# Dealing the keys of a decode attention to the 128 partitions in another order

## The chip, the cores and the metric

The kernel runs on one core of a Trainium2 chip. The metric is the device time of one execution in microseconds (us); the median of three runs before the change is 1363.97 us (1363.89 to 1364.12). The time after the change is compared with it.

## What is computed

One token goes through a layer norm, and then through attention over a long cache and a gated feed-forward block side by side; both results are added to the token. All is float32. Cut to what matters:

```python
# x: [1, 1, 576]; 32 heads of 128; the caches hold 16384 keys a head
xn = layernorm(x)                                    # eps 1e-5
q = (xn @ wq).reshape(1, 1, 32, 128).transpose(0, 2, 1, 3)
scores = einsum("bhqd,bhkd->bhqk", q, k_cache) * 128 ** -0.5
o = einsum("bhqk,bhkd->bhqd", softmax(scores), v_cache)
a = o.transpose(0, 2, 1, 3).reshape(1, 1, 4096) @ wo
b = (gelu(xn @ w_gate) * (xn @ w_up)) @ w_down       # 576 -> 4608 -> 576
out = x + a + b
```

k_cache and v_cache are [1, 32, 16384, 128]. A head's K is 16384 x 128 x 4 bytes = 8.39 MB, and so is its V; 32 heads make 536.87 MB of the 587.6 MB that the kernel reads. In memory the 16384 keys of a head lie one behind the other, 512 bytes each.

Neither the softmax nor the sum over keys asks which key lies in which partition: every order is as good as another, as long as K and V of a head are dealt in the same way.

## The kernel before, in words

**Slots.** Three buffers of 128 partitions x 16384 floats (64 KB in each partition, 8.39 MB in all) hold everything that is streamed: slot_a and slot_b (`sa`, `sb`) take the K of odd and even heads in turn, slot_v (`sv`) takes V. Before the heads they hold the weights of the projections, and after them w_down and wo.

**The deal of the keys.** With P = 128 and R = 16384 / 128 = 128, line 176 makes the views `kv` and `vv` of the caches, in which partition p holds the keys 128p to 128p + 127, that is a block of 128 keys or 64 KB that is contiguous in memory. The block of partition p + 1 follows it. One transfer (lines 352 and 355) moves one head's K or V: 128 blocks of 64 KB, one into each partition.

**One head.** VectorE multiplies the whole K in place by q, which stands in all partitions (line 396), and sums each key's 128 products (line 398), which gives the scores as 128 x 128: partition by key within the block. Then come the maximum (lines 387 to 389, with a transpose on TensorE at line 375), the exponential on ScalarE (line 427) and 32 matmuls of 128 x 512 over V (issued by `chain`, line 337), in which TensorE sums over the partitions. ScalarE takes the result out of PSUM (line 420).

**The order of the transfers.** SyncE (SP) issues all of them from one queue. After the weights of the projections it issues head 0's K in two halves of 64 keys a block (lines 358 and 359, by `load`), then head 1's K and head 0's V, then a loop over pairs of heads. In it, `take` (line 341) waits for a semaphore and lowers it again:

```python
take(nc.sync, s_kf)          # VectorE has read the slot's last K
load_k(i * 2 + (2 + s), dst, s)
take(nc.sync, s_vf)          # TensorE has read the last V
load_v(i * 2 + (1 + s))
```

So a K transfer is issued when VectorE is done with the K two heads back, and a V transfer when TensorE is done with the V before it; SP issues them in just this order, and a wait holds up all that stands behind it. VectorE, ScalarE and TensorE run loops of their own over the heads and meet through semaphores; VectorE's wait for a K of line 396, and TensorE's for V, are for all 16 counts that the 16 DMA engines give when a transfer has landed.

**The end.** While the last two heads are worked on, SP loads w_down and wo into the K slots, and TensorE adds their products up; four small transfers write the 576 outputs.

Of the kernel before, what the change touches and what calls it, by code (L numbers as in the profile page):

```python
# [13 lines left out]
P = 128  # L14
H, SK, DH = 32, 16384, 128
D, DF = 576, 4608
R = SK // P
SUB = 64
# [99 lines left out]
@with_exitstack  # L118
def kernel(ctx: ExitStack, tc: tile.TileContext, x, k_cache, v_cache, wq, wo, wg, wu, wd, out):
    nc = tc.nc  # L120
    ends = tc.alloc_semaphore("ends")
    slots = []
    for i, name in enumerate(("slot_a", "slot_b", "slot_v")):
        t = nc.alloc_sbuf_tensor_at(name, [P, R * DH], F32, offset=SLOT_AT + i * SLOT_B)
        SIZES[t.name] = R * DH
        slots.append(t.ap())
    i = nc.sync.dma_start(slots[0], wq[:DM].rearrange("(p j) f -> p (j f)", j=DJ)).then_inc(ends, 64)
    tc.no_tile_sem_insts.add(i.ins.name)
    tc.add_to_no_dep_group("first", i.ins)
    tc.declare_fence(nc.sync.nop().ins, group="first")  # L130
    with tc.tile_critical(sync_engine=mybir.EngineType.SP):
        decode(tc, x, k_cache, v_cache, wq, wo, wg, wu, wd, out, slots, ends)
    tc.no_sync_barrier()
    nc.sync.wait_ge(ends, 64)
# [19 lines left out]
def decode(tc, x, k_cache, v_cache, wq, wo, wg, wu, wd, out, slots, s_ends):  # L154
    nc = tc.nc
# [4 lines left out]
    def sem():  # L160
        return tc.alloc_semaphore(f"d{next(names)}")
# [11 lines left out]
        SIZES[t.name] = 512 * banks  # L173
        return t.ap()

    kv, vv = (c.rearrange("b h (p n) d -> p (b h) (n d)", p=P) for c in (k_cache, v_cache))
    xf = x.rearrange("b s d -> (b s) d")
    of = out.rearrange("b s d -> (b s) d")
    wmain = {n: w[:DM].rearrange("(p j) f -> p (j f)", j=DJ) for n, w in (("q", wq), ("g", wg), ("u", wu))}
# [4 lines left out]
    sa, sb, sv = slots  # L184
# [34 lines left out]
    def load(dst, src, again=False, **kw):  # L219
        if again:  # L220
            o.dma(dst, src, spent.pop(0), value=32, **kw)
        else:
            s = sem()
            o.dma(dst, src, s, **kw)
            if kw.get("eng") != "scalar":
                spent.append(s)
        return dst
# [13 lines left out]
    for i in range(2):  # L241
# [6 lines left out]
    s_q, s_m, s_n, s_o, s_e, s_v, s_po, s_pq, s_pt, s_pb, s_pc, s_vf, s_kf, s_qf, s_qd, s_d, s_a = (  # L248
        tc.alloc_semaphore(f"h{n}") for n in range(17))
    s_k = [tc.alloc_semaphore(f"k{n}") for n in range(2)]  # L250
# [92 lines left out]
    def head(h):  # L343
        return bass.ds(h, 1)
# [4 lines left out]
    o.wait("scalar", [qb], [z, qs, nb, pe, lsum, oall, qcur])  # L349

    def load_k(h, dst, s):
        nc.sync.dma_start(dst, kv[:, head(h), :].rearrange("p h f -> p (h f)")).then_inc(s_k[s], 16)

    def load_v(h):
        nc.sync.dma_start(sv, vv[:, head(h), :].rearrange("p h f -> p (h f)")).then_inc(s_v, 16)

    parts = [(sb[:, i * SUB * DH : (i + 1) * SUB * DH], S[:, i * SUB : (i + 1) * SUB]) for i in range(R // SUB)]
    for i, (dst, _) in enumerate(parts):
        load(dst, kv[:, 0, i * SUB * DH : (i + 1) * SUB * DH])
    o.wait("sync", [], [sa])  # L360
    load_k(1, sa, 1)
    o.wait("sync", [], [sv])
    load_v(0)
    with nc.sync.Fori(0, (H - 2) // 2) as i:
        for s, dst in ((0, sb), (1, sa)):
            take(nc.sync, s_kf)
            load_k(i * 2 + (2 + s), dst, s)
            take(nc.sync, s_vf)
            load_v(i * 2 + (1 + s))
# [71 lines left out]
    for j in range(1, WD_A):  # L441
        dve("scalar_tensor_tensor", total, first[j], hT[:, j : j + 1], total, op0=ALU.mult, op1=ALU.add)
    take(nc.sync, s_vf)
    load_v(H - 1)
    take(nc.sync, s_kf)
    wd_rows = load_rows(sa, 0, wdv, WD_A, WD_T - WD_A)
# [86 lines left out]
```

## Time and profile before

| | |
|---|---|
| median of 3 runs | 1363.97 us (1363.89 to 1364.12) |
| the profiled execution's own time | 1363.89 us |
| its span, first to last instruction | 1362.1 us |
| time around the span | 1.8 us |
| bytes read from memory | 587.60 MB |
| VectorE (DVE) busy | 1158.7 us, 85% of the span |
| TensorE (PE) busy, modelled | 444.3 us, 33% |
| ScalarE (ACT) busy | 67.8 us, 5% |

The profile is of one execution. It gives each engine's busy time, groups of instructions by source line, what ended an engine's idle time, and for the 16 DMA engines the share of time in which they had a packet under way and the bytes that they moved. A transfer's "us to landing" runs from its issue on SP until its data is there, and so holds the time in which it queued behind earlier transfers.

### The profile page before, as it was taken

How to read it: one execution, taken by the hardware profiler on the slowest of the kernel's cores; microseconds unless marked ns; L12 is line 12 of the kernel's file. 1: busy time of each engine (PE TensorE's matmuls, PEld its weight loads, DVE VectorE, ACT ScalarE, POOL GpSimd, SP SyncE). 2: the span in 40 equal slices, each digit the busy share in tenths (PEclk: the TensorE clock that was granted, in tenths of full speed). 3: DMA queues.
4: the chain of work that ended last, by engine and by line, in shares of the span. 5: the costliest groups of instructions: out<-in, count | busy, mean ns of one | idle time of the engine just before them, and what ended most of it. 6: DMA issues, size and time to landing. Idle time of an engine off the chain costs nothing. (4 is left out here: it accounts for less than half of the span.)

```text
span 1362.1 us, 7778 instructions
## 1 busy us (share of the span) xinstructions
PE 444.3 (33%) x3012; PEld 161.5 (12%) x3012; DVE 1158.7 (85%) x195; ACT 67.8 (5%) x234; POOL 1.0 (0%) x7
## 2 busy tenths in 40 slices
PE   2431233333322333323223333233223333232236
PEld 1110111100110111101111111011011111011012
DVE  1069999999888888899888888998888888988882
ACT  0000000000000000000000000000000000000000
POOL 0000000000000000000000000000000000000000
PEclk9775666666556666666556666665566666655668
DMA  9999999999999999999999999999999999999998
GB/s 401 447 424 435 446 433 435 431 431 433 433 433 431 435 445 435 435 431 431 433 433 433 431 435 445 437 433 431 433 431 433 433 431 435 446 435 433 430 432 349
DMA packets 11827, 587.69 MB, mean 431 GB/s; under 512 B 1319, under 2 KB 1325, under 8 KB 1710
## 3 DMA queue, kind: packets, MB, share of 16 engines
q1 hardware_dynamic: 11812, 587.60, 99.7%
q8 instruction: 5, 0.08, 0.0%
q10 hardware_dynamic: 10, 0.01, 0.0%
HBM read 587.60 MB, written 0.00 MB: 431 GB/s over the span
## 5 line engine op out<-in xcount | busy, mean ns | idle before, releaser
L337 PE MATMUL po<-slot_v,pe 128*4 128x512 f32 x2048 | 292.0, 734 | 580.9 <-PEq L341 580.9
L396 DVE TENSOR_TENSOR slot_a<-slot_a,qs 128x16384 f32<-128x16384 f32 x16 | 275.6, 17226 | 34.9 <-DVEq L341 34.9
L396 DVE TENSOR_TENSOR slot_b<-slot_b,qs 128x16384 f32<-128x16384 f32 x15 | 258.4, 17226 | 32.5 <-DVEq L341 32.5
L398 DVE TENSOR_REDUCE scores<-slot_a 128x128 f32<-128x16384 f32 x16 | 275.5, 17220 | 2.3
L398 DVE TENSOR_REDUCE scores<-slot_b 128x128 f32<-128x16384 f32 x15 | 258.3, 17220 | 2.2
L337 PEld LDWEIGHTS po<-slot_v,pe 128*4 128x4 f32 x2048 | 56.4, 98 | 789.4 <-issue 789.4
L375 PE MATMUL pg<-ident,pm 128*1 128x128 f32 x32 | 11.9, 372 | 238.3 <-PEq L341 238.3
L420 ACT ACTIVATE z<-po 128x512 f32<-128x512 f32 x32 | 19.1, 597 | 831.0 <-ACTq L341 831.0
L337 PE MATMUL pc<-same,z 128*128 128x1 f32 x256 | 59.8, 355 | 0.0
L337 PEld LDWEIGHTS pc<-same,z 128*128 128x128 f32 x256 | 57.1, 328 | 0.5
L210 DVE TENSOR_TENSOR slot_v<-pg,same 128x396 f32<-128x396 f32 (+1 forms) x6 | 3.3, 558 | 52.1 <-PE pg L207 51.9
L375 PEld LDWEIGHTS pg<-ident,pm 128*1 128x1 f32 x32 | 2.5, 79 | 243.6 <-issue 243.6
L389 DVE TENSOR_REDUCE nm<-pg 1x1 f32<-1x128 f32 x32 | 8.9, 279 | 21.5 <-DVEq L341 21.5
L337 PE MATMUL pg<-nm,ones 1*128 1x1 f32 x64 | 17.7, 343 | 18.5 <-PEq L341 18.5
L337 PE MATMUL pqs<-qcur,ones 1*128 1x128 f32 x64 | 14.8, 312 | 25.3 <-PEq L341 25.3
L210 DVE SCALAR_TENSOR_TENSOR slot_b<-slot_b,hT 128x576 f32<-128x576 f32 x27 | 22.1, 819 | 0.9
L337 PEld LDWEIGHTS pg<-nm,ones 1*128 1x128 f32 x64 | 15.9, 307 | 27.9 <-issue 27.9
L425 ACT ACTIVATE nb<-pg 128x1 f32<-128x1 f32 x32 | 5.5, 171 | 240.5 <-ACTq L341 240.5
L210 DVE TENSOR_REDUCE scores<-slot_b 128x64 f32<-128x8192 f32 x2 | 17.4, 8686 | 0.1
L210 DVE TENSOR_TENSOR slot_b<-slot_b,qs 128x8192 f32<-128x8192 f32 x2 | 17.4, 8688 | 0.0
L387 DVE TENSOR_REDUCE pm<-scores 128x1 f32<-128x128 f32 x32 | 9.1, 285 | 8.2 <-DVEq L341 8.0
L337 PEld LDWEIGHTS pqs<-qcur,ones 1*128 1x128 f32 x64 | 9.6, 187 | 53.9 <-issue 53.9
(81 smaller groups left out, 133.6 us busy)
## 6 DMA issues: line engine op xcount, KB each, us to landing
slot_b<-in_A_k_cache_dram SPq DMA_DIRECT2D x2, 4096.0 KB, 24.1
slot_b<-in_B_w_down_dram SPq DMA_DIRECT2D x1, 8064.0 KB, 42.0
slot_b<-in_B_w_gate_dram SPq DMA_DIRECT2D x1, 6912.0 KB, 55.1
slot_a<-in_B_w_up_dram SPq DMA_DIRECT2D x1, 6912.0 KB, 37.8
slot_a<-in_A_wo_dram SPq DMA_DIRECT2D x1, 3456.0 KB, 41.0
slot_v<-in_B_w_gate_dram SPq DMA_DIRECT2D x1, 2304.0 KB, 28.8
slot_v<-in_B_w_up_dram SPq DMA_DIRECT2D x1, 2304.0 KB, 37.2
slot_a<-in_B_w_down_dram SPq DMA_DIRECT2D x1, 2304.0 KB, 28.1
```

Source lines behind the costliest of these rows:

```text
L210: o.op("vector", lambda e: getattr(e, name)(out, *ins, **kw), out, *[a for a in ins if isinstance(a, bass.AP)], *[a for a in kw.values() i ...
L337: i = nc.tensor.matmul(dst, lhs, rhs, start=start, stop=stop)
L375: nc.tensor.transpose(pt[:1, :P], pm, ident).then_inc(s_pt, 1)
L387: nc.vector.reduce_max(pm, sc, axis=AX.X).then_inc(s_m, 1)
L389: nc.vector.tensor_reduce(nm[:1], pt[:1, :P], axis=AX.X, op=ALU.max, negate=True).then_inc(s_n, 1)
L396: nc.vector.tensor_mul(blk, blk, qs.unsqueeze(1).to_broadcast([P, R, DH])).then_inc(s_d, 1)
L398: nc.vector.tensor_reduce(sc, blk, axis=AX.X, op=ALU.add).then_inc(s_d, 1)
L420: nc.scalar.activation(z, PO, AF.Copy).then_inc(s_o, 1)
L425: nc.scalar.activation(nb, pb[:, :1], AF.Copy, scale=SCALE).then_inc(s_a, 1)
```

## The change

The blocks stay what they are, 128 keys or 64 KB contiguous in memory. What changes is the partition into which each goes. The index of a block was the partition p. It is now split as 16j + e, with e from 0 to 15 and j from 0 to 7, and the view has e outside and j inside, so partition 8e + j holds block 16j + e. A transfer's source is now a pattern of 16 (step 64 KB) by 8 (step 1 MB) blocks, where it was one of 128 blocks with a step of 64 KB; its destination is still the slot's 128 partitions in order. Eight partitions that follow one another thus hold blocks 1 MB apart, and 16 partitions with a distance of 8 hold blocks that are neighbours. K and V are dealt alike, so the computation on the chip is the same, with its sums over the partitions in another order. Number and size of the transfers, the waits, the loops and every instruction of the compute engines stay as they were.

```diff
-    kv, vv = (c.rearrange("b h (p n) d -> p (b h) (n d)", p=P) for c in (k_cache, v_cache))
+    kv, vv = (c.rearrange("b h (j e n) d -> e j (b h) (n d)", e=16, j=P // 16) for c in (k_cache, v_cache))
...
     def load_k(h, dst, s):
-        nc.sync.dma_start(dst, kv[:, head(h), :].rearrange("p h f -> p (h f)")).then_inc(s_k[s], 16)
+        nc.sync.dma_start(dst, kv[:, :, head(h), :].rearrange("e j h f -> e j (h f)")).then_inc(s_k[s], 16)
 
     def load_v(h):
-        nc.sync.dma_start(sv, vv[:, head(h), :].rearrange("p h f -> p (h f)")).then_inc(s_v, 16)
+        nc.sync.dma_start(sv, vv[:, :, head(h), :].rearrange("e j h f -> e j (h f)")).then_inc(s_v, 16)
 
     parts = [(sb[:, i * SUB * DH : (i + 1) * SUB * DH], S[:, i * SUB : (i + 1) * SUB]) for i in range(R // SUB)]
     for i, (dst, _) in enumerate(parts):
-        load(dst, kv[:, 0, i * SUB * DH : (i + 1) * SUB * DH])
+        load(dst, kv[:, :, 0, i * SUB * DH : (i + 1) * SUB * DH])
```

## The prediction

> **What bounds the kernel now.** The page's first two parts come first: which engine is busy, and what the DMA engines do beside it.
>
> ```profile
> PE 444.3 (33%) x3012; PEld 161.5 (12%) x3012; DVE 1158.7 (85%) x195; ACT 67.8 (5%) x234; POOL 1.0 (0%) x7
> ...
> DMA  9999999999999999999999999999999999999998
> GB/s 401 447 424 435 446 433 435 431 431 433 433 433 431 435 445 435 435 431 431 433 433 433 431 435 445 437 433 431 433 431 433 433 431 435 446 435 433 430 432 349
> DMA packets 11827, 587.69 MB, mean 431 GB/s; under 512 B 1319, under 2 KB 1325, under 8 KB 1710
> ```
>
> No compute engine is full, and the 16 DMA engines are, in every slice. The second view, the table of windows, puts a number on this for a stretch with weights (30 to 85 us), for the first heads and for the other heads; the last two columns are the DMA engines' busy share and rate.
>
> ```profile
> 30.00:85.00 55.00, 31.20 (x310) 10.47 (x302) 6.52 (x8) 1.97 (x4) 0.00 (x0) 0.81 1.01 436
> 120.00:160.00 40.00, 12.42 (x78) 4.50 (x79) 37.94 (x8) 2.21 (x8) 0.00 (x0) 0.63 0.98 426
> 170.00:1280.00 1110.00, 356.47 (x2233) 127.91 (x2233) 1011.51 (x117) 57.25 (x203) 0.00 (x0) 0.61 1.00 434
> ```
>
> Over 1110 us of heads the engines have a packet under way 1.00 of the time and move 434 GB/s, 27.1 GB/s each. The weights, which lie in memory quite differently, go at 436. A rate that doesn't care what is read is a ceiling of the engines or of the place that they write into, not of the reads.
>
> Third, the timeline, for the length of a head: TensorE starts on a head's V when it lands.
>
> ```profile
> 210.93 9.49 PE L337 MATMUL po<-slot_v,pe 128*4 128x512 f32 x64 [12.52 <-PEq L341]
> ...
> 220.75 0.33 SPq L355 DMA_DIRECT2D slot_v<-in_A_v_cache_dram  x1
> ...
> 231.34 0.33 SPq L352 DMA_DIRECT2D slot_a<-in_A_k_cache_dram  x1
> ...
> 249.53 8.96 PE L337 MATMUL po<-slot_v,pe 128*4 128x512 f32 x64 [14.50 <-PEq L341]
> ```
>
> 249.53 - 210.93 = 38.6 us a head, for 2 x 8.39 MB. So one transfer takes 19.3 us, and one 64 KB row of it, 8 to an engine, takes 19.3 / 8 = 2.41 us. All 32 heads take 32 x 38.6 = 1235 us of the execution's 1363.9; weights and ends make up the other 129.
>
> Fourth, is VectorE close behind? Its groups, and the median times from issue to landing:
>
> ```profile
> L396 DVE TENSOR_TENSOR slot_a<-slot_a,qs 128x16384 f32<-128x16384 f32 x16 | 275.6, 17226 | 34.9 <-DVEq L341 34.9
> L398 DVE TENSOR_REDUCE scores<-slot_a 128x128 f32<-128x16384 f32 x16 | 275.5, 17220 | 2.3
> ...
> L387 DVE TENSOR_REDUCE pm<-scores 128x1 f32<-128x128 f32 x32 | 9.1, 285 | 8.2 <-DVEq L341 8.0
> ...
> slot_v<-in_A_v_cache_dram SPq DMA_DIRECT2D x32, 29.1
> slot_a<-in_A_k_cache_dram SPq DMA_DIRECT2D x16, 42.1
> ```
>
> VectorE works 17.23 + 17.22 us on a head and about a microsecond on the maximum, and waits 34.9 / 16 = 2.2 us for its K: about 36 of 38.6 us. A V transfer is issued 29.1 - 19.3 = 9.8 us before its turn, a K transfer 42.1 - 19.3 = 22.8 us before. The queue is never empty, so the transfers alone set the end.
>
> **The change part by part.** *Removed: reads 512 KB apart.* If an engine moves 8 rows that follow one another, the 16 read at places 512 KB apart, and will read neighbours. By the windows this is worth next to nothing: the heads already go at 434, and the best stretch of any kind at 436. 536.87 MB at 436 take 1231 us in place of 1235, so the gain has a ceiling of 4 us. I take 0, since the DMA share is 1.00 as it is.
>
> [...]
>
> *Added: a third dimension in the source.* Number, length and order of the transfers stay. SP's instruction takes 0.33 us (rows above) for 64 transfers; were it twice as long, SP would spend 21 us more. All of that lies behind the 9.8 us by which V is early, so I take 0; without this cover it would be those 21 us.
>
> *Moved: which engine writes which partitions.* This is the step that I think decides. Before, both sides of a transfer counted 128 equal rows, so the hardware could deal the rows to its 16 engines in any order. Now the source counts 16, then 8. A split over 16 engines that keeps both sides together has one form left: engine e takes the outer index e, which is the partitions 8e to 8e + 7, one after the other. The trace shows what the present deal gives: 16 engines that write at once for 1110 us without holding one another up anywhere. A deal chosen for that need not be this one.
>
> The price has two ends. If the receiving side has no narrow places, it is 0. If it has 16 places as fast as one engine each, a collision-free deal gives each engine a place for itself. Where the partitions of one engine's share lie in two places, and another engine's share in the same two, the pair walks them in step: four rows at the first, four at the second, with half of the 16 places idle. Then a row takes 2 x 2.41 = 4.83 us, a transfer 38.6 us and all heads 2470 us, which is 1235 more. I take this end, for a reason from the rows above: 434 and 436 GB/s from unlike sources say that the ceiling isn't at the reads, and a total that holds so still is what one engine at one place gives.
>
> [...]
>
> *How nearly in step.* If one of a pair leads by x us, it has each place to itself for x, and a transfer (two places) takes 38.6 - 2x. All 16 shares come from one instruction of 0.33 us, so I take x between 0 and 0.33: 64 x 2 x 0.33 = 42 us less at most.
>
> *What is late next.* Nothing else. At 77.2 us a head, VectorE's 36 us lie wholly beside the transfers. SP issues K, V, K, V in a fixed order; with VectorE done 36 us after its K, and V landing 38.6 us after that K, the wait that holds SP is TensorE's for V. V would be issued 9.8 us after the one before landed, when 28.8 us of the K ahead are left, so the queue doesn't run dry. The ends keep their 129 us: the weights' transfers aren't touched.
>
> *Sum*: 1363.9 + 1235 = 2599 us in step, 2557 with the full lead; I take the middle, 2578. The profiled execution (1363.89) is 0.1 us from the median, so nothing is carried over.
>
> **The rivals.**
>
> *Pairs out of step.* Engines drift, and a lead x saves 2x a transfer; at x = 9.65 us (four rows) nothing is lost. x = 4.8 us gives 1363.9 + 64 x (19.3 - 9.6) = 1985 us. For it: nothing makes the engines start a transfer together while the queue is full. Against it: the slowest pair sets every landing, and a pair that runs ahead until its queue is empty starts its next share in step again.
>
> *Not slower: the ceiling is the engines' own.* If 27.1 GB/s is what an engine can do, wherever it writes, then rows dealt otherwise cost nothing: 1364 us. For it: the same rows, since a flat ceiling fits an engine as well as a place. It decides from the point where the receiving side takes two engines at once, 54 GB/s in one place. The same time results if the hardware doesn't deal by the outer 16 at all: then the change doesn't do what it says, and the reads aren't neighbours either.
>
> *A little slower, from the reads.* Each engine's reads now jump by 1 MB. The slowest stretch with heads had 426 GB/s; at 426 in place of 434, 1235 us grow by 23, to 1387 us.
>
> *Faster.* The reads gain the 4 us from above: 1360 us.
>
> **How the numbers follow.** In step, 2450 to 2610 us: 0.62. Partly out of step, 1490 to 2450: 0.18. Unchanged, 1361.3 to 1366.7: 0.12. Slower by less, up to 1490: 0.05. Faster: 0.02; a measurement of this kernel can tell about 0.2%, 2.7 us, from no change, which is most of that ceiling of 4. Over 2610: 0.01. The first two hold 0.80, so the range is 1490 to 2610; the forecast's own is 2450 to 2610. Slower 0.62 + 0.18 + 0.05 + 0.01 = 0.86, same 0.12, faster 0.02. The 0.62 is no more because no row of before shows who owns the ceiling.
>
> **What would show it.** Right: the slices of the heads fall to about 220 GB/s while the DMA share stays near 1.00, since the packets are under way and merely take longer; the weights' slices keep 430 and more. A head takes about 77 us; V lands about 28.8 + 38.6 = 67 us after its issue, K, issued right behind V, about 106. VectorE's groups keep 17.2 us and wait about 41 us a head. Wrong: 434 GB/s in the heads with a head at 38.6 us (the ceiling is the engines'); a rate between, with landings that vary from head to head (out of step); a DMA share well under 1 (the transfers come late, and the waits matter after all).

## The result, and the profile after

The changed kernel takes 2714.61 us (median of four runs, 2706.18 to 2723.54) against 1363.93 us before (four runs): 1.990 times as long, with a 95% interval of 1.988 to 1.993. The forecast was 2578 us, and the range ended at 2610.

The first two parts of the page of after: the compute engines' busy time, then the DMA engines' busy share and their rate in 40 slices.

```profile
PE 416.8 (15%) x3012; PEld 137.5 (5%) x3012; DVE 1158.8 (43%) x195; ACT 67.8 (2%) x234; POOL 1.0 (0%) x7
...
DMA  9999999999999999999999999999999999999996
GB/s 424 227 214 202 215 205 212 210 206 214 206 211 211 206 213 207 210 212 204 215 205 212 211 205 215 206 211 212 204 213 211 207 213 205 212 211 206 214 239 202
DMA packets 11827, 587.69 MB, mean 216 GB/s; under 512 B 1319, under 2 KB 1325, under 8 KB 1710
```

VectorE does the same 1159 us of work. As many packets carry as many bytes, and the DMA engines are as full as before; they move half as much in the same time. Only the first slice, in which the weights come, keeps its rate. The table of windows of after (last columns: DMA share, GB/s):

```profile
85.00:160.00 75.00, 5.82 (x45) 3.50 (x37) 41.46 (x16) 2.17 (x8) 0.00 (x0) 0.53 1.03 216
...
300.00:2600.00 2300.00, 320.73 (x2156) 102.85 (x2156) 1014.06 (x114) 55.27 (x196) 0.00 (x0) 0.55 1.00 209
```

209 GB/s, less than half of 434, at a share of 1.00: each engine always has a packet under way, and a packet takes over twice as long. The trace also keeps the start and the length of every packet, and in the heads one packet is one row of 64 KB. From 300 us on to the last heads, every such packet takes 2.42 us in before and 4.76 to 5.13 us in after, 5.01 in the mean. None comes near the old length. The timeline of after, two V transfers that follow each other, and what SP issues behind them:

```profile
438.95 8.42 PE L337 MATMUL po<-slot_v,pe 128*4 128x512 f32 x64 [67.66 <-PEq L341]
447.62 0.54 SPq L355 DMA_DIRECT2D slot_v<-in_A_v_cache_dram  x1
448.78 0.56 SPq L352 DMA_DIRECT2D slot_b<-in_A_k_cache_dram  x1
...
519.01 9.35 PE L337 MATMUL po<-slot_v,pe 128*4 128x512 f32 x64 [68.41 <-PEq L341]
```

A head takes 519.01 - 438.95 = 80.1 us, so a transfer takes 40.0, where before it was 19.3. V is issued 8.7 us after the one before landed, and K 1.2 us behind V: VectorE is long done, so SP's wait for it has no length. The instruction on SP takes 0.54 us in place of 0.33, with one dimension more in the source; that lies behind the transfers. The groups and the median times to landing of after:

```profile
L396 DVE TENSOR_TENSOR slot_a<-slot_a,qs 128x16384 f32<-128x16384 f32 x16 | 275.6, 17225 | 465.1 <-DVEq L341 465.1
...
L389 DVE TENSOR_REDUCE nm<-pg 1x1 f32<-1x128 f32 x32 | 8.9, 279 | 487.7 <-DVEq L341 487.7
...
slot_v<-in_A_v_cache_dram SPq DMA_DIRECT2D x32, 70.7
slot_a<-in_A_k_cache_dram SPq DMA_DIRECT2D x16, 109.6
```

VectorE now waits twice a head: 465.1 / 16 = 29 us for K, and 487.7 / 32 = 15 us ahead of the maximum. The second is TensorE's order: its transpose for the maximum stands behind the matmuls that wait for V. Neither sets the end.

### The profile page after: what moved, and what is told of

The parts are those of the page before. It is cut to its first block, busy times and chain, and to the rows that moved or that the text cites. A ratio compares the mean times of both kernels' runs of the same rounds, so it can differ in the third digit from the quotient of the medians.

```text
span 2721.8 us, 7778 instructions
## 1 busy us (share of the span) xinstructions
PE 416.8 (15%) x3012; PEld 137.5 (5%) x3012; DVE 1158.8 (43%) x195; ACT 67.8 (2%) x234; POOL 1.0 (0%) x7
## 5 line engine op out<-in xcount | busy, mean ns | idle before, releaser
L396 DVE TENSOR_TENSOR slot_a<-slot_a,qs 128x16384 f32<-128x16384 f32 x16 | 275.6, 17225 | 465.1 <-DVEq L341 465.1
L389 DVE TENSOR_REDUCE nm<-pg 1x1 f32<-1x128 f32 x32 | 8.9, 279 | 487.7 <-DVEq L341 487.7
L337 PE MATMUL pc<-same,z 128*128 128x1 f32 x256 | 42.0, 285 | 0.0
L337 PEld LDWEIGHTS pc<-same,z 128*128 128x128 f32 x256 | 39.3, 234 | 0.5
L337 PE MATMUL pqs<-qcur,ones 1*128 1x128 f32 x64 | 14.8, 312 | 25.4 <-PEq L341 25.4
L337 PE MATMUL pg<-nm,ones 1*128 1x1 f32 x64 | 11.3, 244 | 18.5 <-PEq L341 18.5
L427 ACT ACTIVATE pe<-scores,nb 128x128 f32 x32 | 12.8, 401 | 9.6 <-ACTq L341 9.6
L337 PEld LDWEIGHTS pg<-nm,ones 1*128 1x128 f32 x64 | 9.6, 186 | 23.8 <-issue 23.8
## 6 DMA issues: line engine op xcount, KB each, us to landing
slot_b<-in_B_w_down_dram SPq DMA_DIRECT2D x1, 8064.0 KB, 109.6
```

The source lines that it names most:

```text
L337: i = nc.tensor.matmul(dst, lhs, rhs, start=start, stop=stop)
L389: nc.vector.tensor_reduce(nm[:1], pt[:1, :P], axis=AX.X, op=ALU.max, negate=True).then_inc(s_n, 1)
L396: nc.vector.tensor_mul(blk, blk, qs.unsqueeze(1).to_broadcast([P, R, DH])).then_inc(s_d, 1)
L427: nc.scalar.activation(pe, S[:, bass.ds(i % 2 * R, R)], AF.Exp, bias=nb, scale=SCALE, accum_out=lsum[:, bass.ds(i + h0, 1)]).then_inc(s_e, 1)
```

## The experiments

The theory, "places", is the supposition that the forecast rests on: which partitions are written at the same time sets the rate. Engines that write to one place, as the theory calls it, together get what one of them gets alone, 27.1 GB/s in before, and in the changed kernel pairs of engines do so in step. How many places there are, which partitions make one up, and which engine writes which partitions stands in no record; what the runs show of it are times and rates. The rivals are "reads" (what is read where) and "shape" (a source that counts in two dimensions). All diffs are against the changed kernel unless another is named.

### The deal kept, the reads put back

```diff
-    kv, vv = (c.rearrange("b h (j e n) d -> e j (b h) (n d)", e=16, j=P // 16) for c in (k_cache, v_cache))
+    flat = [c.rearrange("b h s d -> (b h s d)") for c in (k_cache, v_cache)]
+    BK = R * DH
+    kv, vv = (bass.AP(tensor=c.tensor, offset=c.offset, ap=[[9 * BK, 16], [BK, 8], [127 * BK, H], [1, BK]]) for c in flat)
```

> The changed kernel with its deal of partitions kept (outer index 16, so eight consecutive partitions to an engine's share) and its reads put back: the eight blocks of a share follow one another in memory, and the shares lie 576 KB apart (nine blocks, so that the pattern stays one of 16 by 8). A head's blocks then reach into its neighbours', so the keys of a head are not its own. Theory 'places' (pairs of engines write at one place in step): about 2715 us, as after, 80 us a head. Rival 'reads' (neighbouring reads or 1 MB jumps are what slows it): about 1364 us. Rival 'shape' (a source that counts in two dimensions is slow by itself): about 2715. For the open 4% (a head takes 80 us where twice 38.6 is 77): if it is lost where two engines write, the head stays at 80 us; if the 1 MB jumps cost it, the head falls to 77 us and the time to about 2600.

Measured: 2711.07 us (2700.97 to 2717.55), 1.989 times before (1.985 to 1.993). The window of the heads in this kernel:

```profile
300.00:2600.00 2300.00, 312.18 (x2156) 100.18 (x2156) 1014.67 (x114) 55.28 (x196) 0.00 (x0) 0.56 1.00 209
```

The rate is that of after, 209 GB/s, with the eight reads of a share one behind the other and the shares 576 KB apart. "Reads" falls, and the open 4% of the expectation aren't the jumps' either: the rate didn't rise to 217.

### An outer index of 32

```diff
-    kv, vv = (c.rearrange("b h (j e n) d -> e j (b h) (n d)", e=16, j=P // 16) for c in (k_cache, v_cache))
+    kv, vv = (c.rearrange("b h (j e n) d -> e j (b h) (n d)", e=32, j=P // 32) for c in (k_cache, v_cache))
```

> The same idea as the change with an outer index of 32 and an inner one of 4: partition 4a + b holds block 32b + a. Reads of neighbouring groups are neighbours, and an engine's next read is 2 MB on. The source still counts in two dimensions, but a group of four partitions is one outer index, so the 16 engines can get two groups each in any order, as in the kernel before. 'Places': 1364 us (1361 to 1367) if the hardware deals the groups as before, 2715 if it hands out consecutive ones. 'Reads': well over 1364, since reads are still neighbours and the jumps are longer; near 2715 if they cost what they are blamed for. 'Shape': 2715.

Measured: 1363.92 us, ratio 1.000 (0.999 to 1.001). Its window:

```profile
170.00:1280.00 1110.00, 359.15 (x2233) 128.35 (x2233) 1012.75 (x117) 57.20 (x203) 0.00 (x0) 0.61 1.00 434
```

The same reads of neighbours, in the same kind of two-dimensional pattern, at the old 434 GB/s. "Shape" falls. Two things differ from the change: four partitions, not eight, are tied to each other, and a group's next read lies 2 MB on, not 1 MB. The experiment above has shown that the reads don't make the factor of two, so the partitions do. Reads of neighbouring blocks bring nothing that can be measured either: 1363.92 us against 1363.94.

### A pitch of 2 MB

Against the kernel before:

```diff
-    kv, vv = (c.rearrange("b h (p n) d -> p (b h) (n d)", p=P) for c in (k_cache, v_cache))
+    kv, vv = (c.rearrange("b h s d -> (b h s d)").rearrange("(p h f) -> p h f", p=P, h=H) for c in (k_cache, v_cache))
```

> The kernel before, one counting dimension of 128, but with 2 MB from one partition's block to the next in place of 64 KB: head h takes the h-th block of each 2 MB piece of the whole cache, so heads get one another's keys. 'Places' and 'shape': 1364 us (1361 to 1367), as the partitions are dealt as before. 'Reads': clearly slower, since each engine jumps 2 MB with every row and all 16 are at the same offset of a power of two. [...]

Measured: 1373.41 us (1369.68 to 1374.97), ratio 1.006 (1.004 to 1.008).

```profile
170.00:1280.00 1110.00, 355.18 (x2222) 125.73 (x2222) 1004.16 (x114) 56.15 (x198) 0.00 (x0) 0.61 1.00 432
```

So the order of the reads can be measured, at 9.5 us for the largest pitch tried, and it is no factor of two. None of the three theories had this small cost: "places" and "shape" had none, 1361 to 1367 us, and "reads" a clear one, where the loads go at 432 GB/s in place of 434.

### The transfer in two halves

Against the kernel before; K's transfers and the two halves of head 0's K are split likewise, and the two waits count 32:

```diff
...
-        nc.sync.dma_start(sv, vv[:, head(h), :].rearrange("p h f -> p (h f)")).then_inc(s_v, 16)
+        for a in (0, 64):
+            nc.sync.dma_start(sv[a : a + 64], vv[a : a + 64, head(h), :].rearrange("p h f -> p (h f)")).then_inc(s_v, 16)
...
```

> The kernel before with its blocks and its single counting dimension, but each transfer in two: partitions 0 to 63, then 64 to 127. Nothing changes in what is read or in what goes where; a transfer of 64 rows gives each engine four. 'Places': if 64 partitions hold only half of the places, two engines share one all the time: 80 us a head, 2600 to 2750 us, in spite of the old reads. 'Reads' and 'shape': 1364 us, perhaps a few us more for twice the number of transfers. [...]

Measured: 2718.34 us (2717.86 to 2723.45), ratio 1.994 (1.991 to 1.997).

```profile
300.00:2600.00 2300.00, 319.36 (x2156) 102.00 (x2156) 997.11 (x113) 55.28 (x196) 0.00 (x0) 0.55 1.00 208
```

Every block is read from where it was and lands where it did, and the time doubles, as it does with the change. What differs is which partitions are written at the same time, which blocks are read at the same time, and that there are twice as many transfers. The reads made no such difference in the experiments above (209 GB/s where after has 209, 434 and 432 where before has 434), and in the next one four transfers in place of one leave each packet as fast as before, at 2.42 us. That leaves the partitions: transfers of 64 of them go at 208 GB/s here, where those of all 128 went at 434 in before.

### Eight engines with four partitions each

Against the kernel before; K's transfers and head 0's K are split likewise, and the waits count 64:

```diff
-    kv, vv = (c.rearrange("b h (p n) d -> p (b h) (n d)", p=P) for c in (k_cache, v_cache))
+    kv, vv = (c.rearrange("b h (g j e n) d -> g e j (b h) (n d)", g=4, e=8, j=4) for c in (k_cache, v_cache))
...
-        nc.sync.dma_start(sv, vv[:, head(h), :].rearrange("p h f -> p (h f)")).then_inc(s_v, 16)
+        for g in range(4):
+            nc.sync.dma_start(sv[32 * g : 32 * g + 32], vv[g, :, :, head(h), :].rearrange("e j h f -> e j (h f)")).then_inc(s_v, 16)
...
```

> Each transfer in four, of 32 consecutive partitions with an outer index of 8: eight engines work, and an engine's share is four consecutive partitions. [...] If an engine alone keeps its 27.1 GB/s, a head takes 2 x 38.6 = 77.2 us and the time is 2599 us, and the 80.2 us of after are 77.2 plus a loss of 4% from two engines taking turns. If the 4% come from anything else in the use of half of the places, 2700 to 2720 us. [...]

Measured: 2623.52 us (2622.63 to 2624.31), ratio 1.923 (1.920 to 1.927).

```profile
300.00:2400.00 2100.00, 307.93 (x2079) 98.90 (x2079) 950.49 (x109) 53.29 (x189) 0.00 (x0) 0.56 0.50 217
```

Half of the engines work: the share is 0.50, and by the packets' records eight packets are under way at a time. They move 217 GB/s, 27.1 an engine, and each packet takes 2.42 us, just as before. The sixteen engines of after (209) are together slower than these eight (217), by 3.7%: two of after get 209 / 8 = 26.1 GB/s, one here 27.1. The packets say the same, 5.01 us where twice 2.42 is 4.84. By the theory this is the loss when two share a place; no record shows two engines sharing, and why sixteen get less than eight is open. The whole came out 24 us over the expected 2599, of which 3 are the heads.

### An outer index of 8

```diff
-    kv, vv = (c.rearrange("b h (j e n) d -> e j (b h) (n d)", e=16, j=P // 16) for c in (k_cache, v_cache))
+    kv, vv = (c.rearrange("b h (j e n) d -> e j (b h) (n d)", e=8, j=P // 8) for c in (k_cache, v_cache))
```

> The change with an outer index of 8 and an inner one of 16: eight engines work, each with 16 consecutive partitions, four groups of four. [...] If only the number of engines counted, 2600 us, as with eight engines at places of their own.

Measured: 4820.82 us (two runs, 4779.31 and 4862.34; the window is of the longer).

```profile
300.00:4000.00 3700.00, 291.29 (x2002) 93.17 (x2002) 895.90 (x103) 51.27 (x182) 0.00 (x0) 0.53 0.50 118
```

Again half of the engines, as with the eight engines above, but 118 GB/s in place of 217. The number of engines can't explain it: each moves 118 / 8 = 14.8 GB/s, where there it moved 27.1. If the eight held one another up all the time as the sixteen of after do, a transfer would take twice the 40.1 us of after; that makes an estimate of 1364 + 64 x (80.2 - 19.3) = 5260 us, at 209 / 2 = 104 GB/s. The run came out 8% under it, and the packets show why: between 300 and 4000 us they take 2.42 to 5.32 us, over a third of them less than 4.5, where in after none is under 4.76. So here the engines are held up for a part of the time only; the theory calls it out of step.

### Pairs pushed out of step

Three kernels with the same edit and 2, 3 or 4 rows (shown for 2):

```diff
+    lag, rows = sem(), 2
+    spare = [nc.dram_tensor(f"spare{i}", [12, rows + 1, R * DH], F32, kind="Internal").ap() for i in range(2)]
+    for k in (4, 12):
+        nc.sync.dma_start(spare[k // 12][:k, :rows], kv[:k, :rows, 1, :]).then_inc(lag, 16)
     for i, (dst, _) in enumerate(parts):
...
+    nc.sync.wait_ge(lag, 32)
```

> The changed kernel, with engines pushed out of step once. Ahead of the first K, SP issues two copies from the cache to unused memory: one with 4 outer rows and one with 12, of 2 x 64 KB each, so that the first four engines get both and the next eight get one. If engines 0 to 3 share places with 4 to 7, and 8 to 11 with 12 to 15, each pair is then two rows apart, x = 2 x 2.41 = 4.8 us. Nothing else changes in 2715 us. 'Places in step': a transfer takes 38.6 - 2 x 4.8 = 29 us, 30 with the 4% loss while both share, so 1364 + 64 x (30 - 19.3), some 2000 to 2050 us, if the engines keep their distance. If phase plays no part, or the engines fall back into step: about 2720.

> As with two rows, but 3 x 64 KB to an engine and copy: each pair is three rows apart, x = 7.2 us. 'Places in step': a transfer takes 24.1 us, 24.6 with the loss, and the time is about 1700 us. The first engines are then 14.5 us ahead of the last, which is about what the queue covers, so it may come out up to 100 us higher. If phase plays no part: about 2720.

> The copies once more, with 4 x 64 KB to an engine: each pair starts four rows apart, x = 9.65 us, where one engine writes at the first place while the other is at the second. The shift by two rows was gone after one head, and three rows held in part, in some executions. If being in step draws pairs together only where they share a place, four rows apart is the one other position that can last: near 1364 + 64 x (20 - 19.3), up to 1450 us. But the first engines are then 19.3 us ahead of the last, twice the 9.8 us by which a V transfer is issued early at full rate, so they run out of work and lose part of the lead: then somewhere between 1450 and 2700, and different from one execution to the next. If phase is nothing: 2720.

And the control, with 8 and 16 outer rows (in it, the unused memory is larger to match):

```diff
-    for k in (4, 12):
+    for k in (8, 16):
```

> Control for the two kernels with copies: the copies have 8 and 16 outer rows of 2 x 64 KB, so all 16 engines get one and the first eight another. Engines 0 and 4, 8 and 12 and so on stay in step, although the two halves are now 4.8 us apart. 'Places in step' with the pairs as supposed: 2715 to 2730 us, as after. If any disturbance of the queue's order helps, or if the pairs are others (0 and 8, 4 and 12), about 2000 us, as with two rows.

Measured, four runs of each; where runs of one kernel lie far apart, the range says more than the median:

| kernel | median, us | range, us |
|---|---|---|
| control, 2 rows | 2720.83 | 2711.84 to 2724.67 |
| 2 rows | 2704.33 | 2475.47 to 2712.80 |
| 3 rows | 2475.83 | 2155.42 to 2595.69 |
| 4 rows | 2454.69 | 2281.17 to 2605.84 |

The control is as slow as after (ratio 1.993, 1.989 to 1.996), so a copy by itself helps nothing, nor does a shift between one half of the engines and the other, which it leaves: eight of the 16 counts of a V transfer come some 5 us behind the first. Shifts within the supposed pairs make all eight runs with 3 or 4 rows faster, up to 560 us in one run, with the deal, the reads and the shape of the change: when the engines start against each other is part of the cost. With 2 rows one run of four is much faster, at 2475.47 us; the other three, 2701.57 to 2712.80, can't be told from after. The numbers expected for a shift that lasts were missed by far. The windows of the control, then of the kernel with 2 rows, then of that with 4, at the first K's, the next transfers, and the other heads:

```profile
85.00:115.00 30.00, 0.76 (x2) 0.50 (x2) 11.29 (x8) 0.83 (x2) 0.00 (x0) 0.52 1.01 212
```

```profile
85.00:115.00 30.00, 0.76 (x2) 0.50 (x2) 19.33 (x9) 0.83 (x2) 0.00 (x0) 0.53 1.06 271
115.00:200.00 85.00, 6.36 (x31) 3.06 (x35) 53.85 (x8) 1.33 (x6) 0.00 (x0) 0.50 1.01 210
300.00:2400.00 2100.00, 294.26 (x2002) 94.44 (x2002) 917.24 (x105) 51.32 (x182) 0.00 (x0) 0.56 1.00 210
```

```profile
85.00:115.00 30.00, 1.33 (x10) 0.49 (x2) 6.14 (x10) 0.83 (x2) 0.00 (x0) 0.57 0.99 261
115.00:200.00 85.00, 14.94 (x88) 6.55 (x88) 68.36 (x10) 2.88 (x11) 0.00 (x0) 0.54 1.01 276
300.00:2400.00 2100.00, 318.12 (x2156) 101.11 (x2156) 983.67 (x113) 55.33 (x196) 0.00 (x0) 0.56 1.00 224
```

Out of step the first K's go at 271 and 261 GB/s, where the control has 212 and after 226; with 2 rows the gain is gone after 115 us in this execution, with 4 rows most of it after 200. The packets agree. With 2 rows every packet after 115 us takes 4.76 us or more, as in after. With 4 rows 29% of those between 115 and 200 us take less than 3 us, and none does after 200, though a fifth still take less than 4.5. The DMA share is 1.00 throughout, so the engines in front didn't lose their lead by running out of work, which had been the expected way. They lose it while they work; why is open. No record shows a pair by itself. All 16 together aren't drawn back: with 2 rows the 16 counts of a V transfer come in over 18 us at the first head and over 20 at the 30th, where in before they come within 2.

## Why the prediction was right in its cause and wrong in its size

*What bounds the kernel*: right. The transfers set the end in both kernels, and no other engine is late in after (DMA share 1.00, VectorE busy for 43%).

*Reads*: right at 0. Neighbouring reads by themselves give 1363.92 us, and no gain was there to have. That the reads of before lie 512 KB apart was an assumption about which rows an engine moves, and no run shows it.

*Moved partitions*: right, and with the price at the end that was taken. The partitions make it: 209 GB/s with the deal kept and the reads put back, 208 with the old reads in transfers of 64 partitions, 434 with an outer count of 32. The 16 places, the two places of a share and the pairs that walk them were the author's supposition, and no run shows them. What the runs show in their place: eight engines with four partitions each move 27.1 GB/s each, and of the sixteen in after two together move 26.1.

*The failed step* is the price of a transfer, "a row takes 2 x 2.41 = 4.83 us, a transfer 38.6 us", and with it the upper bound of the range, 2610. It holds only if two engines that hold each other up lose nothing beyond that. After moves 3.7% less than the eight engines do, where the forecast has the two equal: a row takes 5.01 us and a transfer 40.1. No row of before could show this loss, and the range had no room for it. The timelines of before and after, at the first V and at the one of the 30th head:

```profile
133.67 8.87 PE L337 MATMUL po<-slot_v,pe 128*4 128x512 f32 x64 [7.46 <-PEq L341]
...
1254.11 2.74 PE L337 MATMUL po<-slot_v,pe 128*4 128x512 f32 x12 [19.20 <-PEq L341]
```

```profile
198.55 9.15 PE L337 MATMUL po<-slot_v,pe 128*4 128x512 f32 x64 [58.90 <-PEq L341]
...
2525.77 1.89 PE L337 MATMUL po<-slot_v,pe 128*4 128x512 f32 x8 [68.49 <-PEq L341]
```

Over 29 heads a head takes (2525.77 - 198.55) / 29 = 80.25 us, where before it was (1254.11 - 133.67) / 29 = 38.64. That is 40.1 a transfer, 1.5 over the 38.6 of the forecast, and 64 x 1.5 = 96 us in all.

*The lead within a pair*, 0 to 0.33 us with the middle taken, was worth 21 us off the sum. No run shows a lead within a pair, and no gain from one shows: no packet of the heads of after took less than 4.76 us.

*The ends*, "keep their 129 us", were short. The profiled execution's span grew by 2721.8 - 1362.1 = 1359.7 us. Of these, 64.9 lie before the first V, 1206.8 in the 29 heads, and 88.0 behind, where three transfers are left (3 x 20.8 = 62 us more). So some 25 us came at the end. In the kernel with the deal kept and the reads put back that stretch is 22 us shorter, with the same rate in the heads, so they aren't a fixed part of the change. Its 30th V, in a span of 2699.2 us:

```profile
2525.22 2.74 PE L339 MATMUL po<-slot_v,pe 128*4 128x512 f32 x12 [67.86 <-PEq L343]
```

The trace shows where they come from. In after, the last two of the 16 counts of a V transfer drift away from the others while the heads go on: the counts come in over 4.7 us at the first V, 10.8 at the 30th and 26.9 at the last. With the reads put back it is 4.3 us, 4.3 and 6.4. So two engines of after fall behind, and the end waits for them. Why they do is open. The three terms together, 96 + 21 and what is left for the ends, about 20 in the median execution, lead from 2578 to 2715.

*What is late next*: right, no wait. V to landing was forecast at 67 and K at 106 us, and came as 70.7 and 109.6, 3 to 6% more. VectorE's wait of 41 us a head came as 29 + 15, in two places where the prediction had one.

*The rivals.* Out of step didn't happen by itself in the change (no packet under 4.76 us), and where it was forced it lasted only in small part (224 GB/s after 300 us with 4 rows, 210 with 2). That the ceiling is the engines' own, wherever they write, falls by the 209 GB/s. Slower by the reads alone, at 23 us, is no part of the change, whose rate stays at 209 GB/s without the jumps; with a pitch of 2 MB the reads cost 9.5 us.

## What to carry to other kernels

A transfer's outer counts decided more here than how many engines work: with 8 the DMA share fell to 0.50, and with 16 it stayed at 1.00, as busy as ever, while the rate was halved. Read the rate beside the share; 1.00 at 209 GB/s where 434 is known meant that packets took longer, 5.01 us for 2.42, not that the load had grown. Transfers over all 128 partitions with an outer count of 128 or 32 kept the full rate here, 434 GB/s; 16, at 209, or two transfers of 64 partitions, at 208, did not. And when a price is "twice", a loss on top of it, here 3.7%, belongs into the range as well.

## What the runs showed of the hardware that wasn't expected

Two of the sixteen engines of after got 26.1 GB/s together, one of the eight with four partitions each 27.1. Engines pushed out of step lost the gain within 40 us (2 rows, the profiled execution) or most of it within some 120 (4 rows) although they never ran out of work (DMA share 1.00). And 2 MB between the rows of a load cost only 0.6%.
